# Hourglass attention feeding a tanh-shrink layer: pooled V read to 80 partitions, more filler matmuls, a last token tile in three pieces

## The chip, the cores and the metric

The kernel runs on one core of a Trainium2 chip. The metric is the device time of one execution in microseconds (us), lower is better; a kernel's time is the median of several executions. A profile is one further execution recorded instruction by instruction. Its span runs from the first to the last instruction and is a little shorter than the time of that same execution.

## The reference

Eight batches, eight heads, 576 tokens and head dimension 64, all float32. Attention is computed twice and added: once on sequences averaged in groups of four tokens (144 tokens, the result repeated four times), and once locally, where a token sees only the tokens less than four positions away. The sum, laid out as 4608 tokens by 512 features, goes through two dense layers.

```python
q_d, k_d, v_d = (t.reshape(B, H, S // 4, 4, D).mean(axis=3) for t in (q, k, v))
out_up = np.repeat(sm_attn(q_d, k_d, v_d), 4, axis=2)
scores = np.where(np.abs(pos[:, None] - pos[None, :]) < 4, scale * q @ k.T, -1e9)
x = out_up + softmax(scores) @ v        # then (B, H, S, D) -> (B * S, H * D)
h = x @ w_in                            # 512 -> 2048
out = (h - np.tanh(h)) @ w_out          # 2048 -> 512
```

## The kernel before, in words

Two heads form a pair, so there are 32 pairs, four to a batch. For a pair, q and k are loaded (`load_qk`, L317) and cast to bf16 (L490), transposed on TensorE (pairs 0 to 7, L520) or by a DMA transpose (L495), averaged in groups of four (L537, L543, L550), multiplied into scores (L559, L582), put through exp (L606, L618, L621), multiplied with V (L634, L640), normalised (L653, L655), and transposed into `xT`, the features-by-tokens input of the dense layers (L666 and L669, or the DMA transpose of L672 with the adds of L684 and L688).

The dense layers go by batch. `mm1` (L718) multiplies `xT` with `w_in` into a bank of PSUM (L727), ScalarE takes tanh (L738), VectorE subtracts (L741) into `gT`. `mm2` (L749) multiplies `gT` with `w_out` (L763): 16 matmuls accumulate one tile of 128 tokens by 512 columns, in four parts of four; then the tile is copied out of PSUM (L778) to one of three `y` buffers and SyncE issues the write to memory (L782). For the last batch the fifth token tile is done in two pieces of 256 columns, so that its last copy and write are smaller. `dense` (L787) merges the steps of `mm1` of one batch with those of `mm2` of the batch before, by even fractions; `dense(B)`, the last call, has only steps of `mm2`.

Nothing is issued in the order of this text. `Program` (L17) records each operation with an engine, a cost, what it reads and writes, and a priority. `order` (L65) goes forward in planned time and gives each engine the ready operation of the lowest number; dense matmuls have number 5000, so they fill the time in which attention has nothing for TensorE. Each engine then runs its own list strictly in that order, and the order between engines is kept by semaphores. `choice` (L59) leaves an operation to whichever of several engines comes free first in the plan.

`emit` (L146) writes the list out. Before the first dense matmul it also looks for planned idle time on TensorE (`idle`, L124): where more than 350 ns lie between two TensorE operations and a PSUM bank is unused, it puts `filler` matmuls (L927) of 128 by 512 zeros in front of the second one. Their number is 0.75 of the free time divided by 430 ns where the second operation is planned before 6000 ns, and by 230 ns otherwise. They compute nothing that is used.

V comes in twice. `load_v` (L351) loads it per head in overlapping windows of 128 tokens for the local part. For pairs 16 to 31 (`DIRECT` is 16) `load_pool` (L364) loads V of a pair a second time, into one of two `vp` buffers: four tokens of 64 values are one row of 256 values, and the pair's 288 rows go to 72 partitions in four blocks (KP is 72). One DMA on SyncE's queue does it (L370), 288 pieces of 1 KB. GpSimd then adds the four tokens in two steps, `vp` (L386) and `vd` (L391); L640 uses `vd`.

SyncE's queue carries all loads, DMA transposes and writes in planned order; loads from pair 12 on also wait for the transposed result of five pairs before (`GATE`, `BEHIND`).

Of the kernel before, what the change touches and what calls it, by code (L numbers as in the profile page):

```python
# [8 lines left out]
FP32 = mybir.dt.float32  # L9
# [6 lines left out]
class Program:  # L16
# [129 lines left out]
    def emit(self, banks=None, end=None, filler=None):  # L146
        order = self.order()
        fill = {}
        if filler:
            until = min(self.start[i] for i in range(len(self.ops)) if end in self.touch[i])  # L150
            self.uses = {name: sorted(
                (self.start[i], self.start[i] + self.ops[i][1] + 200, i in self.fresh)
                for i in range(len(self.ops)) if self.touch[i] & set(keys))
                for name, keys in banks.items()}
            for i, name, room in self.idle(order, banks, until):
                slow = 430 if self.start[i] < 6000 else 230
                fill[i] = (name, int(0.75 * room / slow))
        for i in order:
            if i in fill:
                filler(*fill[i])  # L160
            if self.ops[i][2] is not None:
                self.ops[i][2]()
# [3 lines left out]
def kernel(  # L166
# [9 lines left out]
    nc = tc.nc  # L176
    B, H, S, D = q.shape
    Dm, Dff = moe_w_in.shape
    NTOK = B * S
    NP = H // 2  # L180
    NPAIR = B * NP
# [9 lines left out]
    GW, KP = 32 * NT, G // 2  # L191
# [8 lines left out]
    def fixed(name, shape, dt, n=None, pool=const):  # L200
        if n is None:
            return pool.tile(shape, dt, name=name, tag=name)
        return [pool.tile(shape, dt, name=f"{name}{i}", tag=f"{name}{i}")
                for i in range(n)]

    NQKN, NVST, NVW, NVP = 4, 5, 3, 2
# [12 lines left out]
    qr = fixed("qr", [2 * G9, A9, 2, D], BF16, 2)  # L219
    qk = fixed("qk", [128, 2, S], BF16, 2)  # L220
    qT = fixed("qT", [128, A9, 2 * G9], BF16, 2)
    vp = fixed("vp", [KP, 4, 4 * D], FP32, NVP)
    half = fixed("half", [128, 2, G, 2], FP32)
    qkd = fixed("qkd", [128, 2, GW], BF16, 2)
    E = fixed("E", [128, 1904], BF16, 2)
# [86 lines left out]
    def load(ns, fn, keys, cost, pri, eng="SP", behind=()):  # L312
        op(eng, ns, fn, reads=behind, writes=list(keys) + [("q", keys[0])] +
           [("queue", eng)] * (pri > -30 + 0.1 * INORDER), pri=pri)
        op("DMA", cost, None, reads=[("q", keys[0])], writes=keys, pri=pri)
# [48 lines left out]
    def load_pool(p):  # L364

        b, j, n = p // NP, p % NP, p % NVP
        base = v[b, 2 * j]

        def issue():
            nc.sync.dma_start(out=vp[n], in_=bass.AP(  # L370
                tensor=base.tensor, offset=base.offset,
                ap=[[4 * D, KP], [KP * 4 * D, 4], [1, 4 * D]]))
        load(650, issue, [("vp", n)],
             T_P, -30 + 0.06 + 0.1 * p, behind=[("sent", p - BEHIND)])

    def sum_v(p):

        n, w, jj = p % NVP, (p // 2) % NVW, p % 2
        first = p < DIRECT + 2 * NVW
        t = vp[n]  # L380
        if first:
            op("DVE", 70, lambda: V.memset(vd[w][0:KP, jj, :, 64:65], 4.0),
               writes=[("vd", w)], pri=10 * p - 12)

        def add1(eng):
            eng.tensor_tensor(out=t[:, :, 0:128], in0=t[:, :, 0:128],  # L386
                              in1=t[:, :, 128:256], op=ALU.add)

        def add2(eng):
            with nc.allow_low_precision("pooled v"):  # L390
                eng.tensor_tensor(out=vd[w][0:KP, jj, :, 0:64],  # L391
                                  in0=t[:, :, 0:64], in1=t[:, :, 64:128], op=ALU.add)
        for n1, fn, to in ((1240, add1, ("vp", n)), (710, add2, ("vdd", w, jj))):
            P.choice([("POOL", n1, lambda fn=fn: fn(GP))],
                     reads=[("vp", n)] + [("vd", w)] * first, writes=[to], pri=10 * p - 8)
# [312 lines left out]
    def take():  # L708
        slot = next(x for x in slots if x not in held)
        slots.remove(slot)  # L710
        slots.append(slot)
        return slot

    def span(kb):

        return (kb * S, 512, 1) if kb % 2 == 0 else (kb * S - 64, 320, 2)
# [32 lines left out]
    def mm2(kb, i):  # L749
        ts, part, g = i // 4, i % 4, kb % 2  # L750
        c0, c1 = 0, Dm
        if kb == 0 and i < 4 * HOLD:
            ts, part = i % HOLD, i // HOLD
        if kb == B - 1 and i >= 16:
            ts, c0, c1 = 4, (i - 16) // 4 * (Dm // 2), (i - 12) // 4 * (Dm // 2)
        if part == 0:
            ycur[ts] = take()
            held.append(ycur[ts])
        slot = ycur[ts]

        def mm(e):
            for fc in range(4 * part + 2 * e, 4 * part + 2 * e + 2):
                T.matmul(ps_hy[slot][:, 0:c1 - c0], gT[g][:, fc, ts * 128:ts * 128 + 128],  # L763
                         w_out_sb[:, fc, c0:c1],
                         start=(fc == 0), stop=(fc == N_FF - 1))
        for e in range(2):
            op("PE", 432 * (c1 - c0) // Dm, lambda e=e: mm(e),
               reads=[("w_out", part, c) for c in range(4)] +
               [("gT", g, fc) for fc in range(4 * part, 4 * part + 4)],
               writes=[("hy", slot)], pri=5000)  # L770
        if part == 3:
            held.remove(slot)
            slots.remove(slot)
            slots.append(slot)
            ys = yn[0] % 3
            yn[0] += 1
            P.choice([(eng, ns * (c1 - c0 + 128) // 640,
                       lambda fn=fn: fn(out=y[ys][:, 0:c1 - c0], in_=ps_hy[slot][:, 0:c1 - c0]))  # L778
                      for eng, ns, fn in YOUT],
                     reads=[("hy", slot)], writes=[("y", ys)], pri=-1)  # L780
            r0 = span(kb)[0] + ts * 128
            op("SP", 600, lambda: nc.sync.dma_start(  # L782
                out=out[r0:r0 + 128, c0:c1], in_=y[ys][:, 0:c1 - c0]),
               reads=[("y", ys)], writes=[("yq", ys)], pri=-60)
            op("DMA", 1000, None, reads=[("yq", ys), ("y", ys)], pri=-1)

    def dense(kb):  # L787

        n1 = 16 * span(kb)[2] if kb < B else 0
        n2 = 16 + 4 * ((kb - 1) % 2) + 4 * (kb == B) if kb else 0  # L790
        lead = LEAD if kb == 1 else 0.0
        steps = sorted([(lead + (1 - lead) * (i + 0.5) / n1, 0, i) for i in range(n1)] +
                       [((i + 0.5) / n2, 1, i) for i in range(n2)])
        for _, second, i in steps:
            if second:
                mm2(kb - 1, i)
            else:
                mm1(kb, i)
# [82 lines left out]
    for g in range(2):  # L881
        t = gT[g].rearrange("p f c -> p (f c)").bitcast(FP32)
# [76 lines left out]
```

## Time and profile before

| | |
|---|---|
| time, median of 3 runs | 325.82 us (325.22 to 327.45) |
| time of the profiled execution | 325.69 us |
| its span | 323.7 us |
| TensorE busy | 313.6 us |
| VectorE, ScalarE busy | 218.9 us, 218.7 us |
| GpSimd busy | 190.2 us |
| bytes moved by DMA | 64.50 MB |

On the page, PE is TensorE's matmul, PEld its weight load, DVE is VectorE, ACT ScalarE, POOL GpSimd and SPq the queue of SyncE, which issues the DMAs. A group's row gives line, engine, operation, the tile written and read with its shape, the count, then busy time and mean duration, and the idle time of the engine just before with what ended it. A matmul's duration includes its way through the array, and the next one starts earlier than it ends: how fast a stream of them goes is read from starts, not from durations.

### The profile page before, as it was taken

The numbers are of one execution on the slowest core, as the hardware profiler recorded it, in microseconds if no ns is written. First come the engines' busy times: TensorE is split into PE (matmuls) and PEld (weight loads), VectorE is DVE, ScalarE is ACT, GpSimd is POOL, SyncE is SP. The second block draws the span as 40 slices with busy tenths as digits, with TensorE's granted clock in tenths as the row PEclk, the third lists the DMA queues.
The fourth block names the chain that finished last, engine by engine and source line by source line (L and its number), as shares of the span: only waits on it lengthen the run. The fifth ranks groups of instructions, "written<-read, shape, count | busy, mean of one in ns | idle before, by whom it ended". The sixth has DMA issues, their size and how long they took to land.

```text
span 323.7 us, 7166 instructions
## 1 busy us (share of the span) xinstructions
PE 313.6 (97%) x2648; PEld 174.3 (54%) x2648; DVE 218.9 (68%) x395; ACT 218.7 (68%) x381; POOL 190.2 (59%) x262
## 2 busy tenths in 40 slices
PE   6898999999899999999999999999999999999996
PEld 2464555556654445666654444666654445566544
DVE  7898785678966589787785777777765554554311
ACT  3755886699877976898768877888786334545300
POOL 5658966278656897988887988889844000000000
PEclk9999999999999999999999999999999999999999
DMA  6999999989999899999999999999522211001022
GB/s 198 300 396 334 368 306 343 216 208 233 242 232 202 210 254 225 242 256 251 251 230 284 242 257 212 250 241 284 121 63 61 63 46 52 34 32 34 33 84 79
DMA packets 114515, 64.50 MB, mean 199 GB/s; under 512 B 92848, under 2 KB 97712, under 8 KB 114480
## 3 DMA queue, kind: packets, MB, share of 16 engines
q1 hardware_dynamic: 114480, 64.05, 79.9%
q8 instruction: 20, 0.33, 0.5%
q14 instruction: 15, 0.12, 0.1%
HBM read 42.47 MB, written 9.44 MB: 160 GB/s over the span
## 4 chain that ended last, share of the span: by engine, by line
PE 86%; SPq 5%; DMA 3%; DVE 2%; POOL 1%; issue 1%; ACT 1%; POOLq 0%; ACTq 0%
PE ps_hy L763 38%; PE ps_hy L727 36%; DMA gT<-in_moe_w_in_dram 3%; PE ps_ox L559 3%; PE ps_ox L634 3%; SPq L325 2%; SPq L358 2%; PE ps_ox L640 2%; PE ps_ox L582 1%; PE ps_ox L669 1%; DVE ln L655 1%; PE ps_ox L666 1%; PE ps_ox L520 1%; POOL w_in_sb L417 1%; DVE E L610 1%
## 5 line engine op out<-in xcount | busy, mean ns | idle before, releaser
L727 PE MATMUL ps_hy<-xT,w_in_sb 128*128 128x320 bf16 (+1 forms) x768 | 148.2, 326 | 1.1 <-DVE gT L741 1.1
L763 PE MATMUL ps_hy<-w_out_sb,gT 128*128 128x512 bf16 (+1 forms) x592 | 144.9, 373 | 0.0
L741 DVE TENSOR_TENSOR gT<-ps_hy,u 128x320 bf16<-128x320 f32 (+1 forms) x192 | 103.2, 553 | 61.0 <-ACT u L738 59.0
L738 ACT ACTIVATE u<-ps_hy 128x320 f32<-128x320 f32 (+1 forms) x192 | 92.2, 495 | 49.5 <-PE ps_hy L727 42.6
L727 PEld LDWEIGHTS <-w_in_sb 128*128 128x128 bf16 x768 | 71.8, 98 | 53.9 <-issue 1.5
L763 PEld LDWEIGHTS <-gT 128*128 128x128 bf16 x592 | 56.2, 98 | 53.3
L503 ACT COPY qk<-qT 128x576 bf16<-128x576 bf16 x44 | 52.4, 1208 | 0.0
L537 POOL TENSOR_TENSOR half<-qk 128x576 f32<-128x576 bf16 x29 | 33.3, 1147 | 27.5 <-ACT qk L503 18.9
L490 POOL CAST qr<-qkn 128x576 bf16<-128x576 f32 x51 | 34.4, 690 | 8.1 <-DMA qkn<-in_k_dram 4.6
L655 DVE TENSOR_TENSOR ln<-ps_ox,r 128x896 bf16<-128x896 f32 x32 | 34.9, 1091 | 1.0
L606 ACT ACTIVATE E<-ps_ox 128x912 bf16<-128x912 f32 x28 | 26.1, 932 | 5.0 <-PE ps_ox L559 4.0
L424 POOL CAST vw<-vst 128x640 bf16<-128x640 f32 x32 | 25.0, 781 | 3.8 <-DMA vst<-in_v_dram 3.5
L778 DVE COPY y<-ps_hy 128x512 f32<-128x512 f32 (+1 forms) x20 | 13.3, 663 | 16.7 <-PE ps_hy L763 16.5
L386 POOL TENSOR_TENSOR vp<-vp 72x512 f32<-72x512 f32 x16 | 20.3, 1270 | 1.0 <-DMA vp<-in_v_dram 1.0
L625 POOL TENSOR_TENSOR E<-E,mask 128x240 bf16<-128x240 bf16 x20 | 12.8, 641 | 11.6 <-ACT E L618 10.2
L634 PE MATMUL ps_ox<-vw,E 128*128 128x65 bf16 x320 | 19.6, 194 | 0.0
L634 PEld LDWEIGHTS <-E 128*128 128x128 bf16 x320 | 16.2, 98 | 5.6 <-DVE E L610 0.3
L621 ACT ACTIVATE E<-ps_ox 72x576 bf16<-72x576 f32 (+1 forms) x28 | 18.8, 671 | 0.0
L601 DVE TENSOR_TENSOR ps_ox<-ps_ox,bias 128x912 f32<-128x912 f32 x16 | 17.7, 1109 | 1.5 <-PE ps_ox L559 1.4
L640 PE MATMUL ps_ox<-vd,E 128*128 128x65 bf16 (+1 forms) x256 | 18.3, 193 | 0.1
L559 PEld LDWEIGHTS <-qk 64*128 64x128 bf16 x320 | 9.1, 94 | 15.5 <-issue 11.3
L778 ACT COPY y<-ps_hy 128x512 f32<-128x512 f32 x17 | 10.0, 587 | 7.1 <-PE ps_hy L763 7.1
(83 smaller groups left out, 266.6 us busy)
## 6 DMA issues: line engine op xcount, KB each, us to landing
vst<-in_v_dram SPq DMA_DIRECT2D x64, 160.0 KB, 4.2
qkn<-in_q_dram SPq DMA_DIRECT2D x32, 288.0 KB, 4.3
qkn<-in_k_dram SPq DMA_DIRECT2D x32, 288.0 KB, 4.3
out_dram<-y SPq DMA_DIRECT2D x35, 256.0 KB, 2.5
vp<-in_v_dram SPq DMA_DIRECT2D x16, 288.0 KB
gT<-in_moe_w_in_dram SPq DMA_DIRECT2D x4, 1024.0 KB, 11.0
xT<-in_moe_w_out_dram SPq DMA_DIRECT2D x8, 256.0 KB, 5.1
gT<-in_moe_w_out_dram SPq DMA_DIRECT2D x2, 1024.0 KB, 8.5
```

The lines of the kernel that those rows point to most:

```text
L424: P.choice([(eng, ns, lambda fn=fn: fn(out=vw[w][:, 2 * jj:2 * jj + 2, :, 0:64], in_=vst[s])) for eng, ns, fn in CAST_V[p >= NEARLY]], rea ...
L490: P.choice([(eng, ns, lambda dst=dst, srt=srt, fn=fn: fn(out=dst, in_=srt)) for eng, ns, fn in (any3[2:] if p >= CASTS else any3[:1] + any ...
L503: fn(out=full[:, i].rearrange("p (g a) -> p g a", a=A9), in_=qT[s][:, :, i::2].rearrange("p a g -> p g a"))
L537: eng.tensor_tensor(out=half, in0=four[:, :, :, 0:2], in1=four[:, :, :, 2:4], op=ALU.add)
L606: op("ACT", 820, lambda: A.activation(out=e1, in_=ps[:, :, 0:456], func=AF.Exp, scale=SCALE), reads=ts, writes=[("E", s, 0)], pri=pri)
L634: T.matmul(po[:, hh, 65 * t:65 * t + 65], E[s][:, c:c + 128], vw[w][:, 2 * jj + hh, t, :], start=True, stop=True)
L640: T.matmul(po[:, hh, o:o + 65], E[s][0:kp, c + gw * i:c + gw * i + 128], vd[w][0:kp, jj, 2 * hh + i, :] if direct else vd[w][:, i, 2 * jj ...
L655: op("DVE", 1010, lambda: V.tensor_tensor(out=ln[s].rearrange("p n (h d) -> p h n d", d=D), in0=blocks[:, :, :, 0:64], in1=r[s].unsqueeze( ...
L727: T.matmul(ps_hy[slot][:, 0:n], w_in_sb[:, dc, fc * 128:(fc + 1) * 128], xT[dc][:, t0 + c0:t0 + c0 + n], start=(dc == 0), stop=(dc == N_DC ...
L738: op("ACT", 90 + 76 * n // 100, lambda: A.activation(out=u[us][:, 0:n], in_=ps_hy[slot][:, 0:n], func=AF.Tanh), reads=[("hy", slot)], writ ...
L741: op("DVE", 70 + 105 * n // 100, lambda: V.tensor_tensor(out=gT[g][:, fc, c0:c0 + n], in0=ps_hy[slot][:, 0:n], in1=u[us][:, 0:n], op=ALU.s ...
L763: T.matmul(ps_hy[slot][:, 0:c1 - c0], gT[g][:, fc, ts * 128:ts * 128 + 128], w_out_sb[:, fc, c0:c1], start=(fc == 0), stop=(fc == N_FF - 1))
```

## The change

Three edits. First, `vp` has 80 partitions, and the DMA of `load_pool` reads 80 rows in each of its four blocks instead of 72, for pairs 16 to 30; the eight rows behind each block are the first eight of the next one (or of the next pair), and land in partitions 72 to 79. The last pair keeps 72 rows. `sum_v` takes partitions 0 to 71 as before. Second, the number of fillers: where the next operation is planned before 7000 ns, one for each 430 ns of free time up to eight, and one more for each 220 ns beyond 3300 ns; later, 0.8 of the free time divided by 220 ns. The list has 21 fillers in place of 16. Third, the last token tile is computed, copied and written in pieces of 256, 128 and 128 columns instead of 256 and 256, each with 16 matmuls, a copy and a DMA of its own; `dense(B)` has 28 steps in place of 24.

```diff
             for i, name, room in self.idle(order, banks, until):
-                slow = 430 if self.start[i] < 6000 else 230
-                fill[i] = (name, int(0.75 * room / slow))
+                if self.start[i] < 7000:
+                    fill[i] = (name, int(min(8, room / 430) + max(0, room - 3300) / 220))
+                else:
+                    fill[i] = (name, int(0.8 * room / 220))
...
-    vp = fixed("vp", [KP, 4, 4 * D], FP32, NVP)
+    vp = fixed("vp", [80, 4, 4 * D], FP32, NVP)
...
+        rows = 80 if p < NPAIR - 1 else KP
...
-            nc.sync.dma_start(out=vp[n], in_=bass.AP(
+            nc.sync.dma_start(out=vp[n][0:rows], in_=bass.AP(
                 tensor=base.tensor, offset=base.offset,
-                ap=[[4 * D, KP], [KP * 4 * D, 4], [1, 4 * D]]))
+                ap=[[4 * D, rows], [KP * 4 * D, 4], [1, 4 * D]]))
...
-        t = vp[n]
+        t = vp[n][0:KP]
...
-            ts, c0, c1 = 4, (i - 16) // 4 * (Dm // 2), (i - 12) // 4 * (Dm // 2)
+            ts, c0, c1 = 4, (0, 256, 384)[(i - 16) // 4], (256, 384, 512)[(i - 16) // 4]
...
-        n2 = 16 + 4 * ((kb - 1) % 2) + 4 * (kb == B) if kb else 0
+        n2 = 16 + 4 * ((kb - 1) % 2) + 8 * (kb == B) if kb else 0
```

## The prediction

> **What bounds the kernel now.** I read the page's busy times and chain first, then the busy time by stretches, then who waited for whom, and last the timeline of the two ends of the span, because two of the three edits lie there.
>
> The page, its first part and its chain:
>
> ```profile
> span 323.7 us, 7166 instructions
> ...
> PE 313.6 (97%) x2648; PEld 174.3 (54%) x2648; DVE 218.9 (68%) x395; ACT 218.7 (68%) x381; POOL 190.2 (59%) x262
> ...
> PE 86%; SPq 5%; DMA 3%; DVE 2%; POOL 1%; issue 1%; ACT 1%; POOLq 0%; ACTq 0%
> ```
>
> TensorE is the path. Outside it the chain holds a few per cent, and where they lie decides the worth of each edit. The view of busy time by stretches; the columns are TensorE, its weight loads, VectorE, ScalarE, GpSimd, then granted clock, DMA share and GB/s:
>
> ```profile
> 0.00:10.00 10.00, 6.67 (x46) 2.87 (x48) 7.07 (x38) 3.91 (x6) 5.61 (x19) 1.00 0.78 226
> 10.00:20.00 10.00, 8.77 (x137) 5.53 (x136) 8.77 (x13) 8.65 (x14) 5.69 (x7) 1.00 1.03 326
> ...
> 97.00:232.00 135.00, 135.00 (x1180) 75.33 (x1179) 101.27 (x168) 108.15 (x181) 116.94 (x153) 1.00 1.07 238
> 232.00:303.27 71.27, 71.27 (x457) 38.87 (x456) 37.89 (x68) 38.79 (x75) 8.97 (x13) 1.00 0.17 50
> 303.27:323.70 20.43, 17.31 (x97) 9.21 (x94) 4.11 (x7) 0.48 (x2) 0.00 (x0) 1.00 0.21 78
> ```
>
> From 97 to 232 us, where the pooled V is loaded, TensorE is busy 135.00 of 135.00 us. It has gaps in the first 20 us, and at the end it stops some 3 us before the span does (20.43 - 17.31). So an edit can move the time in three ways only: in the start-up, in the last 3 us, or by making TensorE wait where it does not wait now.
>
> **Edit 1, pooled V on 80 partitions.** It adds no instruction: 16 loads, 16 and 16 additions stay, and the additions still work on 72 partitions. Each of 15 loads grows from 288 to 320 pieces of 1 KB, so 15 x 32 = 480 KB more in a stretch that moves 238 GB/s. The group rows of the load's issue and its first addition, the two rows of waits (all engines, 97 to 232 us) that name loads of V, and the page's row for the load:
>
> ```profile
> L370 SPq DMA_DIRECT2D vp<-in_v_dram x16: 350/531/1132, 97.9 to 221.3; - x16
> L386 POOL TENSOR_TENSOR vp<-vp x16: 1266/1270/1275, 106.7 to 229.5; 72x512 f32<-72x512 f32 x16
> ...
> POOL vw L424 <- DMA vst<-in_v_dram: 2.3, 1, 2.3
> ...
> POOL vp L386 <- DMA vp<-in_v_dram: 1.0, 1, 1.0
> ...
> vp<-in_v_dram SPq DMA_DIRECT2D x16, 288.0 KB
> ```
>
> The addition waited for its load once in 16 times, 1.0 us. GpSimd, which waits, has 135 - 116.94 = 18 us of slack in the stretch, and TensorE, which would have to be reached through GpSimd and the attention behind it, never waits. A load that lands later must first use up that slack; one that lands sooner gives back at most the 1.0 us, to an engine that is not the path. On SyncE's queue the load is one issue as before (0.35 to 1.13 us); behind it stand the next loads and transposes. I take 0. The bounds: below, -1.0 us, if the one wait reaches the end; above, 480 KB at 238 GB/s, that is +2.0 us, if the DMA engines, at a share of 1.07, set the pace and TensorE had to wait for all of it.
>
> **Edit 2, five more fillers.** The timeline of the first microseconds (start, duration, instruction; in brackets the idle time before it and what ended it):
>
> ```profile
> 1.25 3.17 PE L927 MATMUL ps_ts<-lT 128*128 128x512 bf16 x7 [1.25 <-DVE lT L845]
> ...
> 2.51 0.15 PEld L927 LDWEIGHTS <-lT 128*128 128x128 bf16 x1 [0.28 <-issue]
> ...
> 2.94 0.15 PEld L927 LDWEIGHTS <-lT 128*128 128x128 bf16 x1 [0.28 <-issue]
> ...
> 3.79 0.63 PE L927 MATMUL ps_ts<-lT 128*128 128x512 bf16 x1
> 5.64 0.44 PE L520 MATMUL ps_ts<-ident,qr 128*128 128x128 bf16 x5 [1.22 <-POOL qr L490]
> ...
> 6.14 0.59 PE L927 MATMUL ps_ts<-lT 128*128 128x512 bf16 x2
> ...
> 7.78 0.82 PE L927 MATMUL ps_ts<-lT 128*128 128x512 bf16 x3
> 9.20 0.44 PE L520 MATMUL ps_ts<-ident,qr 128*128 128x128 bf16 x5 [0.60 <-DVE qr L490]
> ...
> 21.54 0.38 PE L927 MATMUL ps_ox<-lT 128*128 128x512 bf16 x1
> ...
> 32.24 0.68 PE L520 MATMUL ps_ox<-ident,qr 128*128 128x128 bf16 x9 [0.74 <-POOL qr L490]
> ```
>
> Seven fillers stand in the first gap. Seven means a planned gap of 7 x 430 / 0.75 = 4013 ns to 8 x 430 / 0.75 = 4587 ns. The new rule gives min(8, ...) = 8 plus 713/220 to 1287/220, in sum 11 to 13. So four to six of the five net fillers stand there, and the later gaps gain or lose one at most.
>
> The weight loads of the first fillers are 0.43 us apart (2.51, 2.94), so the seventh, at 3.79, would be followed by an eighth at 4.22. Later ones of 512 columns are 0.21 us apart (x3 in 0.82 at 7.78: the last one takes 0.38 us, as the lone one at 21.54 does, and two starts share the other 0.44). The first gap thus ran at half the later pace, and by 5.64 the chip was at full pace, since five transposes took 0.44 us as at 9.20. From 4.22 on, 11 fillers end their stream at 4.22 + 4 x 0.22 = 5.1 us, 13 at 4.22 + 6 x 0.22 = 5.5 us. The transposes behind them wait for the cast by GpSimd until 5.64. All fit: cost 0. That cover is thin: if the fast pace comes only after the last filler, 11 end at 4.22 + 4 x 0.43 = 5.9 and 13 at 6.8 us, and the transposes start 0.3 to 1.2 us late. Behind the transposes on TensorE stands all of attention, with VectorE and ScalarE waiting for its banks. But at 32.24 us TensorE waits 0.74 us for a cast by GpSimd, and the chain up to there is not TensorE's at all:
>
> ```profile
> 16.46 10.99 DMA gT<-in_moe_w_in_dram
> 27.51 0.98 POOL w_in_sb L417 x2
> ...
> 30.43 1.15 POOL half L537
> ...
> 32.91 1.73 PE ps_hy L727 x8
> ```
>
> These rows of the chain run through the load of `w_in` and GpSimd's casts. A start-up shift under 0.7 us is absorbed there; that is also why earlier full pace gains nothing in an execution like this one. One filler more in a later gap costs 0.22 us at most, before the same wait. I take 0; bounds 0 and +1.2 us.
>
> On this point the Trainium skill, page "TensorE: Matmul & The Clock Gate", Part 1, says that the array runs at half clock until one free-running activity window of about 3.4 us has been busy, so that the moment depends on where the window stands when the kernel starts. The 0.43 and 0.22 us above agree with the two clocks; the dependence on the window no row here shows. It makes one rival below.
>
> **Edit 3, the last tile in pieces of 256, 128 and 128 columns.** The timeline of the end, SyncE's last wait, and the group rows of the copies (min/median/max in ns):
>
> ```profile
> 317.13 0.69 DVE L778 COPY y<-ps_hy 128x512 f32<-128x512 f32 x1 [2.76 <-PE ps_hy L763]
> ...
> 318.23 2.35 PE L763 MATMUL ps_hy<-w_out_sb,gT 128*128 128x256 bf16 x20
> 318.45 1.84 PEld L763 LDWEIGHTS <-gT 128*128 128x128 bf16 x17
> 318.87 0.42 DVE L778 COPY y<-ps_hy 128x256 f32<-128x256 f32 x1 [1.05 <-PE ps_hy L763]
> ...
> 320.62 0.43 DVE L778 COPY y<-ps_hy 128x256 f32<-128x256 f32 x1 [1.32 <-PE ps_hy L763]
> ...
> 321.07 0.33 SPq L782 DMA_DIRECT2D out_dram<-y  x1
> ...
> SPq L954 <- DMA out_dram<-y: 1.2, 1, 1.2
> ...
> L778 DVE COPY y<-ps_hy x20: 424/692/693, 58.3 to 320.6; 128x512 f32<-128x512 f32 x18, 128x256 f32<-128x256 f32 x2
> ...
> L763 PE MATMUL ps_hy<-w_out_sb,gT 128*128 128x256 bf16 x32 | 3.7, 272 | 0.0
> ...
> 26.45 0.68 PE L520 MATMUL ps_ox<-ident,qr 128*128 128x128 bf16 x9
> 26.97 1.67 PE L727 MATMUL ps_hy<-xT,w_in_sb 128*128 128x512 bf16 x7
> ...
> DMA to landing us min/median/max: 2.0/2.5/4.5
> ```
>
> Matmuls. The second 256 columns are 16 matmuls now and 32 afterwards. A matmul of 256 columns takes 272 ns, and 20 span 2.35 us, so they start (2.35 - 0.27) / 19 = 0.109 us apart. The nearest rows for 128 columns, each with a weight load of its own, are the transposes of 128 columns: nine from 26.45 to the next matmul at 26.97, 0.058 us apart, and 0.22 us for a lone one (0.68 - 8 x 0.058). The last piece then ends 31 x 0.058 + 0.22 = 2.02 us after the second piece's start, against 15 x 0.109 + 0.27 = 1.91 us. That is +0.1 us, and +0.03 us if they go at half of 0.109 (31 x 0.055 + 0.22 = 1.93). I take +0.07.
>
> Copy. 512 columns take 692 ns, 256 take 425 ns: 1.04 ns a column, so 128 columns take 425 - 133 = 292 ns: -0.13 us on the path. The middle piece's copy starts about 0.9 us (16 x 0.058) before the last one and is done in 0.3 us; it is covered.
>
> Write. One DMA more, SyncE's issue of 0.33 us, falls between the two copies and is covered. The last write is 64 KB instead of 128 KB. It was issued at 321.07, SyncE took 0.33 us for that and then waited 1.2 us, so it landed at least 1.5 us after the issue; 256 KB took 2.0 us at the least. At most 0.5 us for 128 KB more: halving 128 KB saves between 0 and 0.23 us. I take -0.15, nearer to the upper bound, because both rows go down with size. The third piece's buffer is that of the tile whose copy ran at 317.13 (three buffers in turn). It ended at 317.8, its write landed 2.0 to 2.5 us later, at 320.3, so the copy at 320.7 doesn't wait; a write of 4.5 us, the longest, would cost 1.6 us.
>
> Sum of the end: +0.07 - 0.13 - 0.15 = -0.21 us. With edits 1 and 2 at 0, the profiled execution's 325.69 us becomes 325.48, **325.5 us**. That execution is 0.13 us under the median of 325.82, which the three runs' spread of 2.2 us doesn't distinguish. A measurement of this kernel tells about 1% (3.3 us) from no change, far more than any term here.
>
> **The rivals.**
> - Late full pace in some executions (faster). Before, the fillers cover 1.25 to 4.42 us and then TensorE idles 1.22 us; an execution in which that isn't enough for full pace would run its first attention at half pace. The run of 327.45 us, 1.76 us over the profiled one, could be one. The gap filled to 5.1 us or beyond would end that, and the median falls to the lowest run: 325.22 - 0.21 = 325.0 us. For it: one run of three stands out. Against: the one profile shows the pace reached, and a median leaves out one run of three anyway. The skill page's window, named above, is this mechanism.
> - Fillers in the way (slower). If full pace isn't there at 4.2 us, the transposes start up to 1.2 us late; it decides from 0.74 us on, the wait at 32.24. All of it passed on: 325.5 + 1.2 = 326.7 us. Against: the transposes at 5.64 ran at full pace after seven fillers.
> - DMA sets the pace from 97 to 232 us (slower, the other side). The share of 1.07 leaves no room, 480 KB cost 2.0 us, and TensorE waits: 327.5 us. It decides from where GpSimd's 18 us of slack are used up in one place. Against: one wait of 1.0 us in 16 loads. The Trainium skill, "DMA: Bandwidth & Descriptors", on how many engines a DMA uses, says that the count is the largest number up to 16 that divides the outer sizes: 12 for 72 rows, 16 for 80, so the busiest engine would carry 20 pieces instead of 24. No quoted row shows it.
> - Pooled V lands sooner and it matters (faster): at most the 1.0 us of that wait, 324.5 us. Against: TensorE waits for nothing there.
> - Weight loads bind the 128-column pieces (slower). Each takes 98 ns (1.84 us busy for 17 that overlap a little); unhidden, 32 x 0.098 = 3.1 us instead of 1.9, +1.2: 325.5 + 1.2 - 0.1 = 326.6 us. Against: the transposes at 0.058 us load weights each as well. The Trainium skill, clock-gate page, "Back-to-back issue gap", gives about 81 ns a matmul for 128 columns in such a stream; by it the last 32 would take 2.6 us and the sum would be 326.1 us. The trace's 0.058 us differs.
>
> **How the numbers follow.** The sum as worked out 0.72; late pace mended 0.09; fillers in the way 0.06; DMA pace 0.05; V sooner 0.02; weight loads 0.03; none of these 0.03. The range takes in the first three and the weight loads: from 325.0 less 0.2, 324.8, to 326.7 with 0.2 for the spread, 326.9; it leaves out 0.10. Faster by over 1% (under 322.6) needs a gain that no row offers: 0.01. Slower by over 1% (over 329.1) needs the DMA case at nearly twice its price: 0.03.
>
> **What would show it.** Edit 1: PE 135 of 135 us again in the stretch from 97 to 232, no row of TensorE's waits there, the load's row with 320 KB. Edit 2: 11 to 13 fillers in the first gap, starts going from 0.43 to 0.22 us apart within them, transposes still at about 5.6 us. Edit 3: last copy of about 0.29 us, last matmul of L763 within 0.1 us of its old distance to the first dense work, and a wait of SyncE at the end below 1.2 us. I am wrong if TensorE's waits before 97 us grow, or if the chain shows a DMA in the middle.

## The result and the profile after

The changed kernel takes 327.35 us (median of 19 runs, 326.44 to 328.05); the kernel before, in the same session, 325.22 us (19 runs, 324.38 to 327.45). The ratio is 1.0057 with a 95% interval of 1.0046 to 1.0067, so the change costs 1.5 to 2.2 us: inside 1%, and above the forecast range, which ended at 326.9. The profiled execution took 327.7 us. (Of the experiments further down, the one with five small matmuls in the first gap has a disturbed profiled execution, of 331.59 us, which its ratio leaves out, but which its profile figures come from.)

The page of after: span, busy times, chain, the queue that brings instructions, and the load of pooled V.

```profile
span 326.0 us, 7218 instructions
...
PE 316.1 (97%) x2672; PEld 175.8 (54%) x2672; DVE 221.4 (68%) x396; ACT 218.5 (67%) x381; POOL 188.9 (58%) x262
...
q8 instruction: 21, 0.34, 0.5%
...
PE 89%; DVE 7%; ACT 1%; issue 1%; DMA 1%; DVEq 0%; ACTq 0%
...
vp<-in_v_dram SPq DMA_DIRECT2D x15, 320.0 KB, 4.9
```

VectorE's share of the chain rose from 2% to 7%, and the span grew by 2.3 us. TensorE has 24 matmuls more. Sixteen are the tail's, so eight are fillers: 24 in place of 16, of which the first gap got five (7 to 12) and the later gaps three. (The description of the change above says 21 in all. That number is wrong.)

The view by stretches, to be held against 135.00 of 135.00 and 17.31 of 20.43 before:

```profile
97.00:232.00 135.00, 133.54 (x1158) 74.27 (x1157) 101.11 (x166) 106.54 (x177) 115.09 (x151) 1.00 1.06 236
...
305.50:326.00 20.50, 17.35 (x113) 9.51 (x110) 4.27 (x8) 0.48 (x2) 0.00 (x0) 1.00 0.22 78
```

TensorE now has 1.46 us of gaps where it had none. The view of TensorE's waits from 97 to 232 us, empty for before, says what they are:

```profile
PE ps_ox L637 <- DVE E L628: 1.0, 1, 1.0
PE ps_ox L637 <- DVE E L613: 0.5, 1, 0.5
```

TensorE waits 1.5 us for E, the scores after exp, of one pair (pair 15), whose masks VectorE multiplies in (the kernel's L610 and L625, three lines further down in after). The timeline of VectorE and of GpSimd at that place, before:

```profile
121.21 2.14 DVE L610 TENSOR_TENSOR E<-E,mask 128x912 bf16<-128x912 bf16 x1
123.28 0.27 DVE L625 TENSOR_TENSOR E<-E,mask 128x240 bf16<-128x240 bf16 x1
...
122.20 0.66 POOL L490 CAST qr<-qkn 128x576 bf16<-128x576 f32 x1
125.15 0.73 POOL L424 CAST vw<-vst 128x640 bf16<-128x640 f32 x1 [2.29 <-DMA vst<-in_v_dram]
125.83 1.27 POOL L386 TENSOR_TENSOR vp<-vp 72x512 f32<-72x512 f32 x1
```

The timeline of VectorE, GpSimd and TensorE, after:

```profile
121.70 2.81 DVE L613 TENSOR_TENSOR E<-E,mask 128x912 bf16<-128x912 bf16 x1
124.43 1.35 DVE L628 TENSOR_TENSOR E<-E,mask 128x240 bf16<-128x240 bf16 x1
...
122.70 0.66 POOL L493 CAST qr<-qkn 128x576 bf16<-128x576 f32 x1
123.31 0.72 POOL L427 CAST vw<-vst 128x640 bf16<-128x640 f32 x1
123.99 1.65 POOL L389 TENSOR_TENSOR vp<-vp 72x512 f32<-72x512 f32 x1
...
124.57 0.30 PE L637 MATMUL ps_ox<-vw,E 128*128 128x65 bf16 x4 [0.49 <-DVE E L613]
125.84 0.20 PE L637 MATMUL ps_ox<-vw,E 128*128 128x65 bf16 x1 [0.97 <-DVE E L628]
```

Before, V of pair 18 was late: GpSimd stood idle for 2.29 us ahead of its cast, and in that idle time the masks finished. After, V was there; GpSimd went straight on, and both engines slowed while they worked side by side: the first mask 2.14 to 2.81 us, the second 0.27 to 1.35, and GpSimd's own addition 1.27 to 1.65. The groups of the two masks give the usual durations (minimum, median, maximum in ns), here of before:

```profile
L610 DVE TENSOR_TENSOR E<-E,mask x12: 623/760/2143, 32.7 to 121.2; 128x912 bf16<-128x912 bf16 x12
...
L625 DVE TENSOR_TENSOR E<-E,mask x8: 267/324/791, 35.9 to 123.3; 128x240 bf16<-128x240 bf16 x8
```

So the late load, which looks like a fault in the profile of before, kept GpSimd out of VectorE's way at a place where TensorE soon needs the masks. The second place is the start, in the timeline of TensorE in after:

```profile
1.25 5.30 PE L930 MATMUL ps_ts<-lT 128*128 128x512 bf16 x12 [1.25 <-DVE lT L848]
6.35 0.57 PE L523 MATMUL ps_ts<-ident,qr 128*128 128x128 bf16 x5
...
32.75 0.67 PE L523 MATMUL ps_ox<-ident,qr 128*128 128x128 bf16 x9
```

The first transposes start at 6.35 instead of 5.64 us, behind the fillers, not behind GpSimd. By 23 us the delay has grown to 1.6 us (one group of transposes starts at 24.77 instead of 23.17); by the wait at 32 us most of it is absorbed: 32.75 against 32.24, 0.5 us left. The third is the end, by the timeline of VectorE,

```profile
322.00 0.29 DVE L781 COPY y<-ps_hy 128x128 f32<-128x128 f32 x1 [0.47 <-PE ps_hy L766]
323.05 0.29 DVE L781 COPY y<-ps_hy 128x128 f32<-128x128 f32 x1 [0.77 <-DMA out_dram<-y]
```

and by SyncE's waits:

```profile
SPq L957 <- DMA out_dram<-y: 1.2, 1, 1.2
```

The last copy is short as forecast, but waits 0.77 us for its `y` buffer. From the start of the last matmul to the start of the last recorded instruction it is 3.31 us, against 3.35 before: 0.04 us less, where 0.21 was forecast.

### The profile page after: what moved, and what is told of

It is laid out like the page before. It is cut to its first block, busy times and chain, and to the rows that moved or that the text cites. A ratio compares the mean times of both kernels' runs of the same rounds, so it can differ in the third digit from the quotient of the medians.

```text
span 326.0 us, 7218 instructions
## 1 busy us (share of the span) xinstructions
PE 316.1 (97%) x2672; PEld 175.8 (54%) x2672; DVE 221.4 (68%) x396; ACT 218.5 (67%) x381; POOL 188.9 (58%) x262
## 4 chain that ended last, share of the span: by engine, by line
PE 89%; DVE 7%; ACT 1%; issue 1%; DMA 1%; DVEq 0%; ACTq 0%
PE ps_hy L730 37%; PE ps_hy L766 37%; PE ps_ox L562 3%; PE ps_ox L637 3%; PE ps_ox L643 2%; PE ps_ts L930 2%; DVE E L613 1%; DVE ln L658 1%; PE ps_ox L585 1%; PE ps_ox L672 1%; PE ps_ox L669 1%; DMA out_dram<-y 1%; PE ps_ox L523 1%; DVE gT L744 1%; DVE qk L527 1%
## 5 line engine op out<-in xcount | busy, mean ns | idle before, releaser
L766 PE MATMUL ps_hy<-w_out_sb,gT 128*128 128x512 bf16 (+2 forms) x608 | 144.9, 368 | 0.0
L427 POOL CAST vw<-vst 128x640 bf16<-128x640 f32 x32 | 24.1, 753 | 1.7 <-DMA vst<-in_v_dram 1.7
L781 DVE COPY y<-ps_hy 128x512 f32<-128x512 f32 (+2 forms) x21 | 13.4, 639 | 16.6 <-PE ps_hy L766 15.7
```

The source lines that it names most:

```text
L427: P.choice([(eng, ns, lambda fn=fn: fn(out=vw[w][:, 2 * jj:2 * jj + 2, :, 0:64], in_=vst[s])) for eng, ns, fn in CAST_V[p >= NEARLY]], rea ...
```

## The experiments

The theories: **D**, the loss is the masks of pair 15 slowed by GpSimd, decided by whether V of pair 18 has landed when GpSimd comes to it (about 122.5 us). **F**, fillers in the way: the start-up delay is passed on to the end. For what makes V come sooner: **J**, TensorE's instructions arrive in blocks by DMA, and more TensorE instructions ahead of 120 us move the block that collides with that load. The rivals to D and J are the start-up, the wider load itself, and chance. "Masks" below are the durations of pair 15's two masks in the one profiled execution, "wait" is TensorE's wait for them there, and every ratio is to the kernel before on the same chip.

### Each edit by itself, and two together

Edit 1 alone:

```diff
-    vp = fixed("vp", [KP, 4, 4 * D], FP32, NVP)
+    vp = fixed("vp", [80, 4, 4 * D], FP32, NVP)
...
+        rows = 80 if p < NPAIR - 1 else KP
```

> Edit 1 alone. Theory A (the wider load changes when GpSimd's additions of pooled V run, and near 123 us one then runs beside VectorE's mask of pair 15, whose two instructions grow from 2.14 and 0.27 us to 2.81 and 1.35 us; TensorE waits 1.5 us for them): 1.3 to 2.0 us slower than before, with the waits of TensorE for E in the profile. Rival B (the collision comes from the start-up shift that the fillers make; the wider load is harmless): within 0.4 us of before, no such wait.

Edit 2 alone:

```diff
-                slow = 430 if self.start[i] < 6000 else 230
-                fill[i] = (name, int(0.75 * room / slow))
+                if self.start[i] < 7000:
+                    fill[i] = (name, int(min(8, room / 430) + max(0, room - 3300) / 220))
+                else:
+                    fill[i] = (name, int(0.8 * room / 220))
```

> Edit 2 alone. Theory A: only the start-up shift, 0.3 to 0.7 us slower than before, no wait for E near 123 us. Rival B: 1.8 to 2.5 us slower, the wait near 123 us is there. Rival C (the late full pace in the profile of after was an accident of that execution): within 0.3 us of before.

Edit 3 alone:

```diff
-            ts, c0, c1 = 4, (i - 16) // 4 * (Dm // 2), (i - 12) // 4 * (Dm // 2)
+            ts, c0, c1 = 4, (0, 256, 384)[(i - 16) // 4], (256, 384, 512)[(i - 16) // 4]
...
-        n2 = 16 + 4 * ((kb - 1) % 2) + 4 * (kb == B) if kb else 0
+        n2 = 16 + 4 * ((kb - 1) % 2) + 8 * (kb == B) if kb else 0
```

> Edit 3 alone. Theory A: the last copy waits for a y buffer as in the profile of after (0.17 us late by its matmuls), so the end gains 0.0 to 0.15 us; within 0.3 us of before. Rival: the order of the end costs more, 0.3 us or above slower.

Edits 1 and 3, that is after with the old rule for fillers:

```diff
-                if self.start[i] < 7000:
-                    fill[i] = (name, int(min(8, room / 430) + max(0, room - 3300) / 220))
-                else:
-                    fill[i] = (name, int(0.8 * room / 220))
+                slow = 430 if self.start[i] < 6000 else 230
+                fill[i] = (name, int(0.75 * room / slow))
```

> Edits 1 and 3 without the fillers. Theory A: 1.3 to 2.0 us slower than before, 0.3 to 0.7 us faster than after. Rival B: within 0.4 us of before.

| kernel | median, us (before) | ratio, 95% interval | masks, us | wait, us |
|---|---|---|---|---|
| edit 1 | 325.99 (325.43) | 1.0015, 1.0001 to 1.0029 | 2.79, 1.34 | 1.5 |
| edit 2 | 326.94 (325.43) | 1.0037, 1.0018 to 1.0056 | 2.80, 1.34 | 1.5 |
| edit 3 | 325.86 (325.43) | 1.0017, 0.9996 to 1.0038 | 2.12, 0.79 | 0.4 |
| edits 1 and 3 | 325.67 (325.43) | 1.0002, 0.9984 to 1.0020 | 2.12, 0.27 | 0 |

The fillers carry most of the loss; without them the change costs 0.1 us, -0.5 to 0.7. Theory A, which put the collision down to the wider load, is wrong: edit 1 costs 0.0 to 0.9 us instead of 1.3 to 2.0, and edit 2, for which it expected no wait for E, has one of 1.5 us. Rival B comes nearer, but edit 1's profile has the wait that B ruled out, and edit 2's 0.6 to 1.8 us lie below B's 1.8 to 2.5. Edit 1's one profile shows the slow masks too, but only 2 of its 12 runs lie above 326.5 us, while 10 of edit 2's 12 do: what edit 1 does now and then, edit 2 does nearly always.

### The masks protected, and nothing else changed

If D holds, it is enough to make GpSimd wait. Its cast of V of pair 18 gets an instruction ahead of it that copies two values of pair 15's masked E into a spare tile, so that GpSimd stands until both masks are done; fillers, wide load and tail stay. The same was done to the kernel before.

```diff
+    hold = fixed("hold", [1, 2], BF16)
...
+        def cast(fn):
+            if p == 18:
+                fn(out=hold, in_=E[1][0:1, 912:914])
+            fn(out=vw[w][:, 2 * jj:2 * jj + 2, :, 0:64], in_=vst[s])
...
-                 reads=[("vst", s, 0), ("vst", s, 1)],
+                 reads=[("vst", s, 0), ("vst", s, 1)] + [("E", 1, 0), ("E", 1, 1)] * (p == 18),
```

> The kernel after, plus one GpSimd instruction ahead of its cast of V of pair 18: a copy of two values of pair 15's masked E to a spare tile, so that this cast and the pooled addition behind it start only after VectorE's two masks of pair 15. Nothing else moves. Theory D (the masks crawl because GpSimd works beside them, when V of pair 18 has landed in time; TensorE waits for them): the masks take 2.2 us or less and 0.3 us, TensorE's wait for E near 124 us goes, 1.2 to 1.8 us faster than after, so 0.0 to 0.7 us over before. Rival E (GpSimd loses as much by waiting as VectorE gains, or the masks are slow by themselves): within 0.5 us of after.

> The kernel before with that same instruction. Theory D: most executions of before have GpSimd waiting for V of pair 18 anyway, so the median moves by 0 to -0.3 us and the slower executions (326.0 us and above, about 10 of 35) become rare. Rival E: slower by 0.3 us or above.

After with the wait: 325.26 us against 325.55, ratio 0.9979 (0.9962 to 0.9996). Before with the wait: 325.14, ratio 0.9984 (0.9972 to 0.9997), its 12 runs from 324.88 to 325.81. The timeline of VectorE and GpSimd, after with the wait:

```profile
120.91 2.14 DVE L618 TENSOR_TENSOR E<-E,mask 128x912 bf16<-128x912 bf16 x1
122.97 0.27 DVE L633 TENSOR_TENSOR E<-E,mask 128x240 bf16<-128x240 bf16 x1
...
123.30 0.17 POOL L431 COPY hold<-E 1x2 bf16<-1x2 bf16 x1 [0.75 <-DVE E L633]
123.43 0.71 POOL L432 CAST vw<-vst 128x640 bf16<-128x640 f32 x1
124.10 1.26 POOL L390 TENSOR_TENSOR vp<-vp 72x512 f32<-72x512 f32 x1
```

V of pair 18 is there (the cast follows at once), the masks take 2.14 and 0.27 us, TensorE waits for no E, and the whole loss is gone with everything of the change still in place. That shows the first half of D, that the masks beside GpSimd are the loss. Where the profiled executions part can be read from one kind of TensorE work that is the same in all of them, the transposes of a pair's result (L666 in before); the table has the start of four such groups, in us:

| place | before | after | after with the wait |
|---|---|---|---|
| start-up | 23.17 | 24.77 | 23.97 |
| behind the wait at 32 us | 41.94 | 42.44 | 41.66 |
| ahead of the masks | 89.54 | 90.03 | 89.24 |
| behind the masks | 126.64 | 128.87 | 126.33 |
| end of the span | 323.7 | 326.0 | 323.5 |

Against before, after has lost 0.5 us by the start-up and 1.7 more at the masks, and nothing anywhere else. The two ratios, 1.0057 and 0.9979, lie 2.5 us apart; in the profiles of after without and with the wait, 0.8 us of the difference is there at 23 us already, long ahead of these masks (full pace came at 6.6 and at 6.1 us), so it is not the wait's doing; 1.7 us fall at the masks. The kernel before gains as well: its runs of 326 to 327.8 us vanish, as they would if they were executions in which V of pair 18 came in time; no profile of such a run shows it.

The second half of D, that V's landing decides, fits 14 of the 15 profiles without the wait: where GpSimd stands waiting for V of pair 18, the first mask takes 2.12 to 2.14 us, and where it doesn't, 2.78 to 2.81. The exception is the kernel without fillers in the first gap, further down: V is there, but it is GpSimd's cast that is slow, 1.13 us instead of 0.72, and the first mask keeps its 2.12:

```profile
120.87 2.12 DVE L610 TENSOR_TENSOR E<-E,mask 128x912 bf16<-128x912 bf16 x1
...
122.45 1.13 POOL L424 CAST vw<-vst 128x640 bf16<-128x640 f32 x1
```

The second mask takes 1.34 us or more only where GpSimd's addition of pooled V runs beside it, so that load's landing has a say too.

### The tail with a buffer more

```diff
-    y = fixed("y", [128, Dm], FP32, 3)
+    y = fixed("y", [128, Dm], FP32, 4)
...
-            ys = yn[0] % 3
+            ys = yn[0] % 4
```

> Edit 3 alone with four y buffers instead of three. Theory: the wait of the last copy for a write to land goes; the last copy starts within 0.05 us of the last matmul's end, and from the last matmul's start to the end of the span it takes 3.0 to 3.15 us (before 3.35, after 3.30). In the median that is 0.1 to 0.3 us, at the edge of what can be seen. Rival: no change there.

Edit 3 with four buffers takes 325.39 us against 325.55, ratio 0.9990 (0.9973 to 1.0007). The timeline of VectorE,

```profile
320.51 0.29 DVE L778 COPY y<-ps_hy 128x128 f32<-128x128 f32 x1 [0.60 <-PE ps_hy L763]
```

and the group of SyncE's writes (issue time in ns):

```profile
L782 SPq DMA_DIRECT2D out_dram<-y x38: 332/378/1016, 59.0 to 321.0; - x38
```

The last copy waits for TensorE alone, so the buffer wait is gone. But from the last matmul's start to the last recorded instruction it is 3.40 us, no less than 3.35, and not the 3.0 to 3.15 expected: the middle piece's write took 1.02 us to issue, and the last write stands behind it in SyncE's queue. In edit 3 alone and in edits 1 and 3 that issue took 0.98 and 1.03 us as well, and the end 3.37 and 3.41. In after it took 0.33 us, at the same 0.75 us behind the write before it; why, no run shows.

### Which fillers, and is it the start-up

No fillers in the first gap; twelve there and the later gaps as before; the three later ones only; and twenty in the first gap, with all of the change and GpSimd's wait:

```diff
-                fill[i] = (name, int(0.75 * room / slow))
+                fill[i] = (name, int(0.75 * room / slow) * (self.start[i] > 6000))
```

> The kernel before without any filler in the first gap. Theory F (start-up delays on TensorE up to about 0.5 us are absorbed before 32 us, so late full pace costs little): within 0.5 us of before although full pace comes at 8 us or later. Rival G (fillers earn their place): 1 us or more slower.

```diff
+                if self.start[i] < 6000:
+                    fill[i] = (name, int(min(8, room / 430) + max(0, room - 3300) / 220))
+                else:
+                    fill[i] = (name, int(0.75 * room / 230))
```

> The kernel before with 12 fillers in the first gap instead of 7, the later gaps as before. Theory D (late fillers shift attention by about 0.5 us against the loads, so that V of pair 18 is nearly always there when GpSimd comes to it and the masks of pair 15 crawl): as fill_only, 0.8 to 1.6 us slower than before, masks of 2.8 and 1.3 us in the profile. Rival H (the three fillers in later gaps do it): within 0.4 us of before.

```diff
+                if self.start[i] < 6000:
+                    fill[i] = (name, int(0.75 * room / 430))
...
+                else:
+                    fill[i] = (name, int(0.8 * room / 220))
```

> The kernel before with only the three fillers more in later gaps, seven in the first. Theory D: within 0.4 us of before. Rival H: 0.8 to 1.6 us slower.

```diff
-                    fill[i] = (name, int(min(8, room / 430) + max(0, room - 3300) / 220))
+                    fill[i] = (name, int(min(8, room / 430) + max(0, room - 3300) / 220) + 8 * (self.start[i] < 6000))
```

> after_order with 20 fillers in the first gap. The transposes start at about 8.0 us instead of 6.2. Theory F (up to about 0.7 us of start-up delay on TensorE is absorbed by the wait near 32 us, more is passed on): 1.0 to 1.8 us slower than after_order, 0.7 to 1.5 us slower than before. Rival (the load of w_in and GpSimd's casts bound the start-up, TensorE has plenty of room): within 0.4 us of after_order.

| kernel | median, us (before) | ratio, 95% interval | first transposes, us | masks, us |
|---|---|---|---|---|
| none in the first gap | 326.05 (325.55) | 1.0020, 1.0001 to 1.0038 | 5.74 | 2.12, 0.79 |
| twelve there | 326.78 (325.55) | 1.0042, 1.0021 to 1.0064 | 5.79 | 2.81, 1.34 |
| the three later ones | 326.32 (325.55) | 1.0033, 1.0010 to 1.0057 | 6.14 | 2.80, 0.27 |
| twenty, with the wait | 326.31 (325.55) | 1.0028, 1.0014 to 1.0042 | 7.86 | 2.16, 0.27 |

The timeline of TensorE, VectorE and GpSimd with twelve fillers in the first gap and nothing else changed:

```profile
1.25 4.71 PE L929 MATMUL ps_ts<-lT 128*128 128x512 bf16 x12 [1.25 <-DVE lT L847]
5.79 0.44 PE L522 MATMUL ps_ts<-ident,qr 128*128 128x128 bf16 x5
...
31.76 0.68 PE L522 MATMUL ps_ox<-ident,qr 128*128 128x128 bf16 x9 [0.42 <-POOL qr L492]
...
120.73 2.81 DVE L612 TENSOR_TENSOR E<-E,mask 128x912 bf16<-128x912 bf16 x1
123.47 1.34 DVE L627 TENSOR_TENSOR E<-E,mask 128x240 bf16<-128x240 bf16 x1
...
122.34 0.72 POOL L426 CAST vw<-vst 128x640 bf16<-128x640 f32 x1
```

At 31.76 us the program is ahead of the kernel before (32.24), and it is still 0.42% slower, with the slow masks: the transposes of the table above start at 41.46 us, 0.5 us earlier than in before, and at 127.90, 1.3 us later. So the start-up isn't what costs: five matmuls in the first 6 us act at 123 us, and H, the three later ones, isn't needed for it. F has its place only further out: with the masks protected, twenty fillers delay the first transposes to 7.86 us and are slower than the changed kernel with the wait, which has twelve, by 1.0 us by the medians, 1.6 by the ratios. No filler in the first gap costs 0.7 us (0.0 to 1.2), between F's 0.5 and G's 1. The three later fillers alone missed the expectation of at most 0.4 us: about 1.1, with runs from 324.88 to 329.54. Their profile shows the first mask slow and a wait of 0.5 us; I have no profile of its slowest runs.

### Why V comes sooner: blocks of instructions

The 20 packets of q8 before carry 0.33 MB, 16.4 KB each. The view of DMA by window has such a packet among the loads: in the kernel before it falls into 119.6 to 122.5 us and not into 116 to 119.6,

```profile
q8 instruction: 1, 0.02, 5.2%
```

and with twelve fillers in the first gap into 116 to 119.6 us and not into 119.6 to 122.5:

```profile
q8 instruction: 1, 0.02, 1.7%
```

In the landing events of the trace (a load is spread over 16 DMA engines), the second half of V of pair 18 was issued at 118.19 us in before; 12 of its 16 parts had landed by 121.53, and four came between 124.03 and 125.03. So more than one engine was late, and J's picture of a single one is too simple. In the kernels with the block sooner, V is there by 123.02 us (in the kernel of twenty fillers, which runs later, by 123.71), and the last part of the output's write issued about 1.1 us ahead of it lands 3.0 to 5.2 us after its issue, against 2.4 to 2.8 in the others. To test J: five matmuls of four columns behind the seven fillers, which add 10 TensorE instructions and next to no time; twelve fillers in the first gap but none later (8 instructions fewer than before); twenty such matmuls; and five of them in the dense layers ahead of the block (63 to 70 us) or behind it (168 to 183 us).

```diff
+        for _ in range(small):
+            T.matmul(tiles[name][:, 0, 0:4], warm[:, 0:128], warm[:, 0:4], start=True, stop=True)
```

> The kernel before with its 7 fillers in the first gap and five matmuls of 4 columns behind them, which end before the transposes start: as many TensorE instructions ahead of 120 us as in fill12 (10 more than before), the start-up in time as before. Theory J (TensorE's instructions come in blocks of 16 KB over the same DMA engines; more instructions ahead bring the block near 120 us forward to about 118 us, one engine is late for an earlier transfer instead of for V of pair 18, and the masks crawl): 0.5 to 1.3 us slower than before, the block's row in the DMA view before 119.6 us as in fill12. Theory D (the fillers work by shifting attention in time): within 0.3 us of before, the block after 119.6 us.

```diff
-                fill[i] = (name, int(0.75 * room / slow))
+                if self.start[i] < 6000:
+                    fill[i] = (name, int(min(8, room / 430) + max(0, room - 3300) / 220))
```

> 12 fillers in the first gap as in fill12, and none in the later gaps: 8 TensorE instructions fewer ahead of 120 us than in before, 18 fewer than in fill12. Theory J: the block comes after 120.3 us, V of pair 18 is late, within 0.4 us of before. Theory D: as fill12, 0.8 to 1.6 us slower.

```diff
-                fill[i] = (name, int(0.75 * room / slow))
+                fill[i] = (name, int(0.75 * room / slow), 20 * (self.start[i] < 6000))
```

> As pad5 with twenty matmuls of 4 columns, 40 TensorE instructions more than before. Theory J: the block comes several us earlier still, near 115 us; whether V of pair 18 is then in time isn't foretold, the time may lie on either side, but the block's place moves on by about 2 to 4 us from pad5's. Theory D: within 0.4 us of before; transposes up to 0.3 us late.

```diff
+            if kb == 1 and dcs[0] == 0 and 2 <= i < 7:
+                T.matmul(ps_hy[slot][:, 0:4], w_in_sb[:, 0, 0:128], xT[0][:, t0 + c0:t0 + c0 + 4],
+                         start=True, stop=True)
```

> The kernel before with five matmuls of 4 columns more between 63 and 70 us, ahead of dense steps whose first matmul overwrites what they write: 10 TensorE instructions more before 120 us, start-up untouched. They cost up to 0.2 us of TensorE by themselves. Theory J (the place of TensorE's instruction block near 120 us decides): as pad5 and fill12, 0.6 to 1.4 us slower than before, block before 119.8 us, masks of pair 15 slow. Theory K (the fillers bring the collision about in another way than by their number): 0.0 to 0.3 us slower, block at 120 us or later.

```diff
+            if kb == 4 and dcs[0] == 0 and 2 <= i < 7:
```

> The same five matmuls between 168 and 183 us, behind the block: 0.0 to 0.3 us slower than before under theories J and K; if it is slower by 0.6 us or more, the number of instructions before 120 us isn't what counts and J falls.

The last: the five ahead of the block and GpSimd's wait together.

> pad_front with the GpSimd instruction of before_order that waits for pair 15's masks. Theories D and J: block before 119.8 us as in pad_front, masks of 2.2 and 0.3 us all the same, 0.0 to 0.5 us faster than before (before_order's 0.4 us less the 0.2 us of the matmuls). If D falls: as pad_front.

| kernel | median, us (before) | ratio, 95% interval | block, us | masks, us |
|---|---|---|---|---|
| five small in the first gap | 326.86 (325.73) | 1.0014, 0.9985 to 1.0043 | 118.1 | 2.79, 1.38 |
| twelve fillers, none later | 326.65 (325.73) | 1.0030, 0.9998 to 1.0063 | 121.5 | 2.79, 0.27 |
| twenty small | 327.28 (325.73) | 1.0039, 1.0016 to 1.0063 | 118.7 | 2.78, 1.35 |
| five ahead | 327.06 (325.95) | 1.0026, 1.0001 to 1.0051 | 117.3 | 2.81, 0.27 |
| five behind | 326.27 (325.95) | 0.9995, 0.9970 to 1.0021 | 121.9 | 2.79, 0.27 |
| five ahead, with the wait | 325.52 (325.95) | 0.9987, 0.9967 to 1.0008 | 118.6 | 2.14, 0.27 |

By the times of these packets in the traces, the block is at 119.8 to 122.0 us in the kernels without added TensorE instructions ahead of it (before 120.4, edit 1 120.4, edit 3 119.8, edits 1 and 3 120.3) and at 117.3 to 119.4 with some (after 119.4, edit 2 118.1, twelve fillers 117.8, the three later ones 117.5), except where twenty fillers made the whole program 1.7 us later (120.5). Small matmuls that compute nothing of use cost 1.3 us when there are twenty; five cost 0.8 ahead of the block and nothing that shows behind it (-1.0 to 0.7); and with GpSimd's wait, the cost ahead is gone. All this is as J says. Against it: the first two rows decide nothing (in the second, 9 of 12 runs show a mean clock of 0.984 to 0.995, where before has at least 0.998, so the lost pace may add time of its own); twenty small matmuls should have moved the block further than five, and didn't; their first transposes start 0.75 us late in the profile, so that some of their 1.3 us may be start-up; and three profiles have a slow first mask and V in time with the block late, edit 1 (120.4), twelve fillers and none later (121.5) and the five behind (121.9). Each kernel has one profile, and those of the five ahead (325.52 us) and the five behind (327.37) lie far from their medians. J is a likely part of the fillers' share, argued and not shown; what else sets V's landing, and why place and count don't go in proportion, stays open.

### The best version

The kernel before with edit 1 and GpSimd's wait, old fillers and tail:

```diff
+        rows = 80 if p < NPAIR - 1 else KP
...
+            if p == 18:
+                fn(out=hold, in_=E[1][0:1, 912:914])
```

> The kernel before with 80 rows of pooled V and the one GpSimd instruction that waits for pair 15's masks; no filler or tail edit. Theory D with edit 1 harmless by itself: 0.2 to 0.6 us faster than before, as before_order (325.14 against 325.55). Rival (the wider load costs or gains by itself): 0.3 us or more away from before_order's ratio of 0.9984.

It takes 325.09 us against 325.55, ratio 0.9983 (0.9968 to 0.9998), runs from 324.54 to 325.73, masks 2.15 and 0.27 us. By the ratios it is 0.1 to 1.0 us faster than before and some 2.4 us faster than after. Before with the wait alone has 0.9984, so the wider load itself brings nothing that shows.

## Why the prediction was wrong

**The bound** was right: TensorE is the path, and the prediction named the three ways to move the time, the third being to make TensorE wait where it did not. That is the one that happened, and no term of the sum stood for it.

**Edit 2 is the step that failed**: "I take 0; bounds 0 and +1.2 us." The count was right for the first gap (12), though the later gaps gained three and not one at most; "that cover is thin" was right (the pace of 0.22 us came at 6.6 us instead of 4.3, the transposes 0.7 us late), and the absorption at 32 us was nearly right (0.5 us left). But the step looked for the effect only up to 32 us. By itself the edit cost 0.37% (0.6 to 1.8 us), and its profile has waits of 1.5 us at 124 us. A row quoted in the prediction, "POOL vw L424 <- DMA vst<-in_v_dram: 2.3, 1, 2.3", was left with GpSimd's slack. The question that would have found it: what runs on the other engines during those 2.3 us, and what happens to it if the wait goes? The group of the masks, 760 ns at the median and 2143 at the most, has its maximum just there.

**Edit 1**: 0 was taken, 0.0 to 0.9 us measured, and none shows with the masks protected. The clause that failed is that a load that lands sooner "gives back at most the 1.0 us": in edit 1's profile pooled V of pair 18 landed at 123.41 us instead of 125.17, the addition ran beside the second mask, and sooner was worse. The upper bound, 2.0 us for 480 KB, didn't come true; TensorE waited for no load.

**Edit 3**: -0.21 us was forecast and -0.1 to 1.2 measured for it alone, so no gain shows. The matmuls (starts 0.056 us apart, 0.055 to 0.058 forecast) and the copy (0.29 us) were right. The write was mis-sized: the last 64 KB landed in 1.60 to 1.65 us against 1.69 for 128 KB, 0.04 to 0.09 instead of 0.15. And "the copy at 320.7 doesn't wait" failed in after: 0.77 us for a write of which one of 16 parts landed 2.85 us after its issue. With that wait gone, in the kernel of four buffers, an issue of 1.0 us takes its place; the sum had 0.33, covered.

**The rivals.** Late full pace mended: no; without any filler in the first gap, or with full pace at 8.8 or 9.9 us (edit 3, edit 1), the program reaches 32 us at 31.9, as early as with it. Fillers in the way: the mechanism is there, for 0.5 us of the 2.3 by which the two profiles differ. DMA pace: 327.5 us comes nearest in number, by a mechanism that isn't there. V sooner matters: it does, with the other sign. Weight loads: no, the matmuls start 0.056 us apart with a weight load each.

## What to carry to other kernels

A late load can protect another engine's work; before you hurry it, look at what runs beside the idle time that it ends, and compare the extremes of a group's durations with its median. Where a critical operation suffers from a neighbour engine, make the neighbour wait on purpose: a copy of two values took back the whole loss, and narrowed the spread of the kernel before. A change of a few instructions early in a long program can act a hundred microseconds later, here by the landing of a load, so a term of 0 for "covered work" needs a bound that includes the far end.

## What the runs showed of the hardware

- VectorE's products of two SBUF tensors and GpSimd's work slow each other: 0.76 to 2.81 us and 0.32 to 1.35 on VectorE, 1.27 to 1.65 on GpSimd. The Trainium skill, page "SBUF — State Buffer", "Who interferes with whom", says that such a VectorE instruction contends with a GpSimd instruction that reads SBUF, that the ports they share are locked by one at a time, and that the order of issue decides who waits. The contention agrees, and either engine can be the one that waits: with no filler in the first gap GpSimd's cast took 1.13 us instead of 0.72, and VectorE's mask kept its 2.12. The lock itself no row shows.
- Instructions come in packets of 16.4 KB, by their count TensorE's. A load issued 2.2 us before one had four of its 16 parts land 2.5 to 3.5 us after the other twelve; that the packet is the reason isn't shown. The Trainium skill, page "Runtime: NRT & Kernel Launch", "Instruction fetch mechanics", gives blocks of 16 KiB or 256 instructions on a queue of the sequencer's own, whose cost is mostly hidden. The size agrees, and so does the count: 20 x 256 instructions is about the 2648 matmuls and 2648 weight loads of the kernel before. Whether a cost fell on other transfers stays open.
- The moment of full pace varies from 4.0 to 12.3 us between the profiled executions. With it at 8.8 and 9.9 us the program still reached the transposes at 32 us at 31.9.
- A load of 80 rows shows 16 landing events, one of 72 rows 12 and one soon after the issue. The Trainium skill's rule in "DMA: Bandwidth & Descriptors", cited in the prediction, has 16 and 12 engines: the counts agree.
- A write of 64 KB issued 0.75 us behind one of 128 KB took SyncE 0.98 to 1.03 us to issue in three kernels and 0.33 us in after.
